# A written order of single steps for the last stage's first tiles, a raw row's scale from its maximum, and column sums moved into the expert products

## The chip, the cores and the metric

One core of one Trainium2 chip runs the whole program in one launch. The metric is the device time of an execution in microseconds. Engines in the text: PE is the matrix engine (its weight loads are shown as PEld), DVE, ACT and POOL work elementwise, SP issues the DMAs.

## The reference

Three computations follow each other. Pooled attention over 8 heads gives `x` (4608 rows of 512). A soft mixture of 8 experts takes `x` to 32 slots, sends each slot through its expert's two layers, and mixes the slots back to rows. The last part, which the change touches, works row by row on that mixture `x`:

```python
h = x @ w_in
e = np.exp(h - h.max(axis=-1, keepdims=True))
solu = h * (e / (e.sum(axis=-1, keepdims=True) + 1e-09))
mu = solu.mean(axis=-1, keepdims=True)
var = ((solu - mu) ** 2).mean(axis=-1, keepdims=True)
return ((solu - mu) / np.sqrt(var + 1e-06) * g_ln) @ w_out
```

`w_in` is 512 by 1024, `w_out` 1024 by 512, both given in double precision.

## The kernel before

**Stages.** Attention with the slot sums takes the program to about 170 us; the second expert layer follows (line L847, sixteen slots of four matmuls, two per expert, each slot waiting for its weights from DMA); then the slots are multiplied with `w_in` once (L893 to L917), so that a row of the last stage needs one short product. The last stage treats the 4608 rows as 36 tiles of 128 rows.

**A tile of the last stage.** PE makes `h` (128 by 1024) from the mixing weights `cS` and the matrix `MS`; DVE finds the maximum `nm`; ACT takes the exponential `e` and its sum; DVE multiplies `u = h * e` and sums it; POOL and ACT work out mean and variance; `u` is brought to its normed form `v`, split into a high and a low f16 part (`vhi`, `vlo`), and laid with the 1024 columns on the partitions. Then PE makes 24 matmuls of 128 by 512 per tile: 8 chunks of `vhi` with `W_hi` and with `W_lo` (L1137, L1138), and 8 of `vlo` with `W_hi` (L1140). `W_hi` and `W_lo` are the two f16 parts of `w_out` with `g_ln`.

**Three kinds of tile.** Tiles 0 to 2 are "raw" (functions `raw_*`): their `u` is turned on PE before mean and variance are known, and the mean's part is put right at the end with the column sums of W. Those sums are made by `out_sums` (L1074, L1075: for each of 8 chunks one matmul of a matrix of ones with `W_hi` and one with `W_lo`) and kept by ACT in `csum`. A raw tile's `u` is scaled to fit f16 by `raw_scale`, which runs two more maximum reductions over `h`, of absolute values (L999), and three operations on one column (L1000 to L1002). Tile 3 is normed first and then turned on PE (L1044 to L1047). From tile 4 on the f16 parts are turned by DMA: SP issues one transposing DMA for `vhi` and one for `vlo` (L1129), and each finished block of three tiles leaves by a 768 KB output DMA (L1159) from the same SP queue.

**What sets the order.** Most of the program is ordered by a scheduler at build time. From the end of the expert products the order is written by hand in the string `steps`: each name is an operation declared with `op` and the names that it needs. In before the steps reach whole functions: `F3` is all of tile 3's front from `h` to its statistics, `G3` its turning, `P0a` both parts of four chunks of tile 0's products. The fixed order holds up to the step `E`; the operations behind it, and all later tiles, are again put in order by the scheduler. The names of the steps: f h's matmul, x maximum, k scale, e exponential, u product with h, t turning on PE, h (with two digits) the high part, w the low part, m mean, v squares, d statistics, P products, R output rows, p S T the copies of M that make `MS`, o column sums; the first digit is the tile, the second the half.

**Dummy matmuls.** Slots 9 to 14 of the expert products are each followed by one matmul of 128 by 512 into a tile that nobody reads (`DUM`, `spare`, L876).

Of the kernel before, what the change touches and what calls it, by code (L numbers as in the profile page):

```python
# [19 lines left out]
P = 128  # L20
# [65 lines left out]
def moe_attention_kernel(ctx: ExitStack, tc, q, k, v, phi, w1, w2, w_in, w_out, g, out):  # L86
# [639 lines left out]
    if True:  # L726
# [114 lines left out]
        DUM = {9: (512,), 10: (512,), 11: (512,), 12: (512,), 13: (512,), 14: (512,)}  # L841
        if DUM:
            spare = psE.tile([P, DM], F32, name="spare")
# [8 lines left out]
        CE = (0, 0, 0, 2, 9, 11, 12, 12, 13)  # L852
        CI = {3: (("o", 2),), 4: (("o", 3),), 6: (("i", 0),), 7: (("i", 1),), 11: (("i", 2),)}
# [29 lines left out]

        t1 = {}
# [67 lines left out]
    BF = dict(e=2, u=3, v=2, h1=2, h2=2, s=4, hi=4)  # L952
# [13 lines left out]
    csum = T_all.rearrange("p g s -> p (g s)")  # L966
# [74 lines left out]
    def split_turned(v, hi, lo, hf):  # L1041
        pu = ps2.tile([P, 4, P], F32, tag="vT", name="vT")
        for c in range(4):
            pe.transpose(pu[:, c, :], v[:, P * c:P * c + P], ident)  # L1044
        hd = hi[:, 4 * hf:4 * hf + 4, :]
        act.activation(hd, pu, AF.Copy)  # L1046
        dve.tensor_tensor(lo[:, 4 * hf:4 * hf + 4, :], pu, hd, ALU.subtract)  # L1047

    def raw_mean(i):
        hs, nm, u, e, st = u_t[i]  # L1050
        y = rs_t[i] = wk2.tile([P, 4], F32, name="y0", bufs=2)
        pool.tensor_tensor(y[:, 0:1], st[:, 2:3], st[:, 3:4], ALU.add)
        pool.tensor_scalar(y[:, 0:1], y[:, 0:1], -1.0 / DF, None, ALU.mult)
# [16 lines left out]
    def out_sums(c):  # L1070
        if c == 0:
            t1["pcs"] = ps2.tile([P, DM], F32, tag="o", name="pcs")
        pcs = t1["pcs"]
        pe.matmul(pcs, ones_h, W_hi[:, c, :], start=(c == 0), stop=False)  # L1074
        pe.matmul(pcs, ones_h, W_lo[:, c, :], start=False, stop=(c == NFC - 1))  # L1075

    def out_sums_kept():
        act.activation(csum, t1["pcs"], AF.Copy)

    def front(i):  # L1080
# [15 lines left out]
        z = wk2.tile([P, 3], F32, name="z", bufs=BF["s"])
# [7 lines left out]
        u_t[i] = u, nmu, sr  # L1104
        r = rs_t[i] = wk2.tile([P, 1], F32, name="r", bufs=BF["s"] + 1)
        pool.tensor_scalar(r, sr[:, 1:2], sr[:, 2:3], ws[:, 2:3], ALU.mult, ALU.mult)  # L1106

    def turn(i):

        u, nmu, sr = u_t.pop(i)  # L1110
        hi, lo = (wk2.tile([P, NFC, P], F16, name=x, bufs=BF["hi"]) for x in ("vhi", "vlo"))
        hi_t[i], lo_t[i] = hi, lo
        v = wk2.tile([P, DF], F32, name="v", bufs=BF["v"])
        if V == "act":
            b = wk2.tile([P, 1], F32, name="b", bufs=BF["s"])
            pool.tensor_tensor(b, nmu, sr[:, 0:1], ALU.mult)  # L1116
            act.activation(v, u, AF.Identity, bias=b, scale=sr[:, 0:1])  # L1117
        else:
            dve.tensor_scalar(v, u, nmu, sr[:, 0:1], ALU.add, ALU.mult)
        if i < NPT:  # L1120
            for hf in range(2):
                split_turned(v[:, 512 * hf:512 * hf + 512], hi, lo, hf)
            return
        v1 = wk2.tile([P, DF], F16, name="v1", bufs=BF["h1"])
        v2 = wk2.tile([P, DF], F16, name="v2", bufs=BF["h2"])
        dve.tensor_scalar(v1, u, nmu, sr[:, 0:1], ALU.add, ALU.mult)  # L1126
        eng[H2].tensor_tensor(v2, v, v1, ALU.subtract)  # L1127
        for src, dst in ((v1, hi), (v2, lo)):
            sp.dma_start_transpose(out=dst, in_=src)  # L1129
# [12 lines left out]
    def rows_out(i):  # L1142
        po = po_t.pop(i)
# [48 lines left out]
    for m in range(NRAW, NT):  # L1192
        for j in range(NRAW + 3, m + LAG + 1) if m == NRAW else (m + LAG,):
            if j < NT:
                front(j)
            if NRAW + 3 <= j - 1 < NT:
                turn(j - 1)
# [59 lines left out]
```

## Time and profile before

| what | value |
|---|---|
| median of 3 runs | 445.54 us (444.97 to 446.08) |
| span of the profiled execution | 444.7 us |
| PE busy in the span | 90% |
| DVE, ACT, POOL busy | 72%, 67%, 52% |
| first matmul of tile 0's `h` | 222.42 us |
| first of tile 0's products | 232.36 us |
| last matmul | about 441.4 us |

The profiled execution is known by its span alone, 444.7 us from the first to the last instruction; the median of the runs is 0.8 us above it. Times in the views count from the span's start. A timeline row gives the start, the length, the instruction and, in brackets, how long the engine stood idle ahead of it and what ended that wait. The ends of matmuls are modelled, so that neighbouring rows overlap: the time that PE needs for one is the distance between starts.

### The profile page before, as it was taken

To read this page: it belongs to the slowest core of one execution; us is meant where nothing else is said; L and a number is where in the kernel's file an instruction comes from. 1 tells how busy PE (TensorE), PEld (TensorE's weight loads), DVE (VectorE), ACT (ScalarE), POOL (GpSimd) and SP (SyncE) were. 2 spreads that over 40 slices of the span, in tenths; PEclk is the share of its full clock that TensorE was granted. 3 is DMA by queue.
4 is the path that set the end of the run, shared out by engine and by line. 5 is a ranking of instruction groups with operands and counts; after the bars stand their busy time and mean duration, and the time that the engine had idled before them with its cause. 6 is when DMAs were issued, how large, how long until landed. Compare 5 with 4: busy or idle time off the path is not lost. (4 is left out here: it accounts for less than half of the span.)

```text
span 444.7 us, 8298 instructions
## 1 busy us (share of the span) xinstructions
PE 398.7 (90%) x2983; PEld 231.1 (52%) x2983; DVE 320.1 (72%) x519; ACT 299.2 (67%) x664; POOL 229.7 (52%) x427
## 2 busy tenths in 40 slices
PE   4679988987999797868789999999999999999997
PEld 4667867866977424321234544444444444444445
DVE  4897897798873624788379887778888887878610
ACT  3588987767795505765338867778887887777721
POOL 5498776568331026773213556665555555555510
PEclk9899998999899887998999999999999999999999
DMA  8999999673779797899300065777765786665661
GB/s 253 412 396 418 398 413 363 228 251 132 277 276 341 260 326 288 330 420 422 151 1 1 16 150 112 150 166 113 172 165 96 177 177 105 147 158 106 151 165 47
DMA packets 87800, 97.07 MB, mean 218 GB/s; under 512 B 70096, under 2 KB 74960, under 8 KB 82768
## 3 DMA queue, kind: packets, MB, share of 16 engines
q1 hardware_dynamic: 87760, 96.55, 69.3%
q8 instruction: 23, 0.38, 0.3%
q14 instruction: 17, 0.14, 0.1%
HBM read 70.32 MB, written 9.44 MB: 179 GB/s over the span
## 5 line engine op out<-in xcount | busy, mean ns | idle before, releaser
L1137 PE MATMUL o<-W_hi,vhi 128*128 128x512 f16 x280 | 106.4, 380 | 1.1 <-ACT vhi L1046 1.0
L1138 PE MATMUL o<-W_lo,vhi 128*128 128x512 f16 x280 | 106.1, 379 | 0.0
L1140 PE MATMUL o<-W_hi,vlo 128*128 128x512 f16 x280 | 67.3, 379 | 0.5 <-DVE vlo L1026 0.5
L366 PE MATMUL sc<-BD,qT 128*128 128x144 f32 x320 | 53.4, 316 | 13.8 <-ACT BD L307 7.8
L366 PEld LDWEIGHTS sc<-BD,qT 128*128 128x128 f32 x320 | 47.3, 212 | 16.3 <-POOL sel L264 6.6
L1117 ACT ACTIVATE v<-u,b,sr 128x1024 f32<-128x1024 f32 x33 | 40.9, 1239 | 15.0 <-POOL b L1116 14.6
L1137 PEld LDWEIGHTS <-vhi 128*128 128x128 f16 x280 | 27.3, 98 | 38.9 <-issue 7.5
L1127 DVE TENSOR_TENSOR v<-v,v 128x1024 f16<-128x1024 f32 x32 | 39.2, 1224 | 10.8 <-ACT v L1117 10.6
L1094 ACT ACTIVATE e<-u,nmu 128x1024 f32<-128x1024 f32 x33 | 37.9, 1148 | 13.4 <-POOL nmu L1093 12.9
L1089 ACT ACTIVATE e<-h,nm 128x1024 f32<-128x1024 f32 x33 | 36.6, 1110 | 13.5 <-DVE nm L1086 13.3
L1140 PEld LDWEIGHTS <-vlo 128*128 128x128 f16 x280 | 27.2, 98 | 33.5 <-DVE vlo L1026 1.0
L405 POOL TENSOR_TENSOR a<-a,rs 128x864 f32<-128x864 f32 x23 | 37.7, 1649 | 13.1 <-DVE rs L403 6.9
L1138 PEld LDWEIGHTS <-vhi 128*128 128x128 f16 x280 | 27.4, 98 | 30.1 <-issue 0.9
L1091 DVE CUSTOM_DVE_ANT_0 u<-h,e 128x1024 f32<-128x1024 f32 x33 | 40.3, 1222 | 3.7 <-ACT e L1089 3.4
L1086 DVE TENSOR_REDUCE nm<-h 128x1 f32<-128x1024 f32 x33 | 40.1, 1220 | 3.9 <-PE h L1083 3.8
L1126 DVE TENSOR_SCALAR v<-u,nmu,sr 128x1024 f16<-128x1024 f32 x32 | 26.0, 812 | 18.8 <-POOL sr L1103 18.7
L411 PE MATMUL pt<-ident,a 128*128 128x128 f32 x180 | 30.8, 287 | 4.5 <-ACT aT L417 3.0
L377 DVE TENSOR_REDUCE nmax<-sc 128x6 f32<-128x432 f32 x48 | 28.1, 597 | 6.4 <-PE sc L366 6.0
L417 ACT ACTIVATE aT<-pt 128x384 f32<-128x384 f32 x60 | 28.0, 491 | 6.7 <-PE pt L411 6.3
L1106 POOL TENSOR_SCALAR r<-sr,ws 128x1 f32<-128x1 f32 x33 | 29.1, 881 | 3.4
L1103 POOL TENSOR_TENSOR sr<-z,exponents 128x3 f32<-128x3 f32 x33 | 28.9, 875 | 2.7
L1153 ACT ACTIVATE ob<-o,r 128x512 f32<-128x512 f32 x32 | 21.4, 669 | 9.6 <-PE o L1140 9.6
(238 smaller groups left out, 764.4 us busy)
## 6 DMA issues: line engine op xcount, KB each, us to landing
w<-in_w_dram SPq DMA_DIRECT2D x16, 1024.0 KB, 10.0
vT<-in_v_dram SPq DMA_DIRECT2D x8, 1152.0 KB, 14.7
out_dram<-ob SPq DMA_DIRECT2D x11, 768.0 KB, 3.7
w<-in_w_dram SPq DMA_DIRECT2D x16, 512.0 KB, 5.7
kT<-in_k_dram SPq DMA_DIRECT2D x7, 1152.0 KB, 13.7
qT<-in_q_dram SPq DMA_DIRECT2D x7, 768.0 KB, 14.3
qT<-in_q_dram SPq DMA_DIRECT2D x8, 384.0 KB, 16.7
raw<-in_w_in_dram SPq DMA_DIRECT2D x3, 1024.0 KB, 9.5
```

The costliest lines, as they stand in the source:

```text
L366: pe.matmul(sc[:, r].rearrange("p h j -> p (h j)"), qT[n][:, hp, x, :], BD[b % NBD][:, hp, :], start=(i == 0), stop=(i == len(hv) - 1))
L405: eng.tensor_tensor(av, av, rs.unsqueeze(3).to_broadcast([P, NR, 4, J]), ALU.mult)
L411: pe.transpose(pt[:, r, :], a_buf[n % NA][:, r, CH[c]:CH[c] + P], ident)
L1086: dve.tensor_reduce(nm, hv, axis=AX.X, op=ALU.max, negate=True)
L1089: act.activation(e, hv, AF.Exp, bias=nm, accum_out=st[:, 0:1])
L1091: dve.tensor_tensor_reduce(u, hv, e, 1.0, 0.0, ALU.mult, ALU.add, st[:, 1:2])
L1094: act.activation(e, u, AF.Square, bias=nmu, accum_out=st[:, 2:3])
L1117: act.activation(v, u, AF.Identity, bias=b, scale=sr[:, 0:1])
L1127: eng[H2].tensor_tensor(v2, v, v1, ALU.subtract)
L1137: pe.matmul(po, hi[:, c, :], W_hi[:, c, :], start=(c == 0), stop=False)
L1138: pe.matmul(po, hi[:, c, :], W_lo[:, c, :], start=False, stop=False)
L1140: pe.matmul(po, lo[:, c, :], W_hi[:, c, :], start=False, stop=(c == NFC - 1))
```

## The change

It has four parts.

1. `out_sums` moves from the last stage into the expert products: chunks 0 to 5 are written behind slots 12, 13 and 14, where the dummy matmuls of these slots go; chunk 6 and 7 and the copy into `csum` become steps between the end of the expert products and the making of `MS`.
2. `raw_scale` takes the scale from the maximum that is already there (`nm`) and not from two reductions of absolute values.
3. The functions of tiles 3 to 9 are cut into single steps (`front_pe`, `front_max`, and so on; the steps `Fa` to `Fg`, `Ga` to `Gy`), the products of tiles 0 to 2 into high parts (`P0a`, `P0b`), which need only `vhi`, and low parts (`P0al`, `P0bl`). A new string `steps` writes out their order up to tile 3's products, where `E` now stands, and the fronts up to tile 9.
4. Three buffers for `e` where two were, three for `y0` where two were.

```diff
-        DUM = {9: (512,), 10: (512,), 11: (512,), 12: (512,), 13: (512,), 14: (512,)}
+        DUM = {9: (512,), 10: (512,), 11: (512,)}
...
+        CS = {12: (0, 1), 13: (2, 3), 14: (4, 5)}
...
                 pe.matmul(spare[:, 0:nn], ident, w2t[x // 2, x % 2, 3][:, 0:nn], start=True, stop=True)
+            for c in CS.get(x, ()):
+                out_sums(c)
...
+        for c in (6, 7):
+            op(f"o{c}", f"o{c - 1}" if c > 6 else "", out_sums, c)
+        op("csum", "o7", out_sums_kept)
...
+        steps = ('a0 o6 a1 s0 s1 s2 s3 o7 so i0 i1 M0 M1 csum N0 mh0 N1 mh1 X '
+                 'f00 f01 p0 S0 x00 x01 k0 p1 e00 e01 S1 T0 u00 f10 t00 u01 h00 t01 h01 T1 P0a w00 x10 m0 f11 w01 x11 k1 e10 e11 P0al '
...
-    BF = dict(e=2, u=3, v=2, h1=2, h2=2, s=4, hi=4)
+    BF = dict(e=3, u=3, v=2, h1=2, h2=2, s=4, hi=4)
...
     def raw_scale(i):
 
         hs, nm, u, e, st = u_t[i]
-        am = wk2.tile([P, 2], F32, name="am", bufs=2)
-        for hf in range(2):
-            dve.tensor_reduce(am[:, hf:hf + 1], hs[hf], axis=AX.X, op=ALU.max, apply_absolute_value=True)
-        dve.tensor_tensor(am[:, 0:1], am[:, 0:1], am[:, 1:2], ALU.max)
-        dve.tensor_scalar(am[:, 0:1], am[:, 0:1], 1e-30, 2.0 ** -14, ALU.max, ALU.mult)
-        dve.reciprocal(st[:, 4:5], am[:, 0:1])
+        am = wk2.tile([P, 1], F32, name="am", bufs=2)
+        dve.tensor_scalar(am, nm, -1.0, nm, ALU.mult, ALU.max)
+        dve.tensor_scalar(am, am, 1.0, 2.0 ** -14, ALU.max, ALU.mult)
+        dve.reciprocal(st[:, 4:5], am)
...
-    def products(i, c0, c1):
+    def products(i, c0, c1, what="hl"):
...
-        for c in range(c0, c1):
+        for c in range(c0, c1) if "h" in what else ():
             pe.matmul(po, hi[:, c, :], W_hi[:, c, :], start=(c == 0), stop=False)
             pe.matmul(po, hi[:, c, :], W_lo[:, c, :], start=False, stop=False)
-        for c in range(c0, c1):
+        for c in range(c0, c1) if "l" in what else ():
             pe.matmul(po, lo[:, c, :], W_hi[:, c, :], start=False, stop=(c == NFC - 1))
...
-        op(f"P{i}a", f"w{i}0", products, i, 0, 4)
-        op(f"P{i}b", f"w{i}1 P{i}a", products, i, 4, 6)
-        op(f"P{i}c", f"P{i}b", products, i, 6, 8)
+        op(f"P{i}a", f"h{i}0", products, i, 0, 4, "h")
+        op(f"P{i}al", f"w{i}0 P{i}a", products, i, 0, 4, "l")
+        op(f"P{i}b", f"h{i}1 P{i}al", products, i, 4, 8, "h")
+        op(f"P{i}bl", f"w{i}1 P{i}b", products, i, 4, 8, "l")
```

**PE, the last slots of the expert products.** `p_2401` is the tile that gathers the expert products, `w_60` to `w_74` the weights of slots 12 to 15, `spare` the dummies, `pcs` the column sums, `ps` the first matmuls behind the experts. Before, the slots and the dummies alternate:

```order
L847 MATMUL p_2401<-w_54_2331,hTm 32x512 x4
L876 MATMUL spare<-w_54_2331,ident 128x512
L847 MATMUL p_2401<-w_60_2335,hTm 32x512 x4
L876 MATMUL spare<-w_60_2335,ident 128x512
L847 MATMUL p_2401<-w_64_2337,hTm 32x512 x4
L876 MATMUL spare<-w_64_2337,ident 128x512
L847 MATMUL p_2401<-w_70_2339,hTm 32x512 x4
L876 MATMUL spare<-w_70_2339,ident 128x512
L847 MATMUL p_2401<-w_74_2341,hTm 32x512 x4
L893 MATMUL ps<-sel_73,s_2620 128x32 x4
```

With the change seven groups like the first four rows here, chunks 0 to 6 of the sums, stand together between the dummy of slot 11 and slot 12 (chunk 7 comes behind `ps`):

```order
L848 LDWEIGHTS ones_h
L848 MATMUL pcs<-W_hi,ones_h 128x512
L849 LDWEIGHTS ones_h
L849 MATMUL pcs<-W_lo,ones_h 128x512
L856 MATMUL p_2401<-w_60_2335,hTm 32x512 x4
L856 MATMUL p_2401<-w_64_2337,hTm 32x512 x4
L856 MATMUL p_2401<-w_70_2339,hTm 32x512 x4
L856 MATMUL p_2401<-w_74_2341,hTm 32x512 x4
L904 MATMUL ps<-sel_73,s_2630 128x32 x4
```

So the scheduler has put the sums ahead of slot 12, also those that the code writes behind slots 12 to 14, and nothing stands between the last four slots.

**DVE, tile 0 in the last stage.** `h_2662` and `h_2663` (now `h_2677` and `h_2678`) are the halves of tile 0's `h`, `pM` the copies of M that make `MS`, ISA is the product `u`. Before:

```order
L985 TENSOR_REDUCE nm_2669<-h_2662 128x1
L1037 TENSOR_TENSOR MS<-pM_2664,MS 64x512
L985 TENSOR_REDUCE nm_2669<-h_2663 128x1
L988 TENSOR_TENSOR nm<-nm_2669 128x1
L1037 TENSOR_TENSOR MS<-pM_2665,MS 64x512
L999 TENSOR_REDUCE am<-h_2662 128x1
L999 TENSOR_REDUCE am<-h_2663 128x1
L1000 TENSOR_TENSOR am<-am 128x1
L1001 TENSOR_SCALAR am<-am 128x1
L1002 RECIPROCAL st<-am 128x1
L1011 ISA u,st<-h_2662,e,st 128x512
```

With the change:

```order
L1004 TENSOR_REDUCE nm_2685<-h_2677 128x1
L1004 TENSOR_REDUCE nm_2685<-h_2678 128x1
L1007 TENSOR_TENSOR nm<-nm_2685 128x1
L1017 TENSOR_SCALAR am<-nm 128x1
L1018 TENSOR_SCALAR am<-am 128x1
L1019 RECIPROCAL st<-am 128x1
L1054 TENSOR_TENSOR MS<-pM_2679,MS 64x512
L1028 ISA u,st<-h_2677,e,st 128x512
L1028 ISA st 128x1
L1028 ISA u,st<-h_2678,e,st 128x512
```

The two reductions into `am` are gone from between the maxima and the first `u`, and of the two operations that make `MS` one stands ahead of the first `u` and one behind the second.

## Rows read from the trace of the kernel before

**Rows 1.** The page, part 1: busy us of each engine, share, instructions.

```profile
PE 398.7 (90%) x2983; PEld 231.1 (52%) x2983; DVE 320.1 (72%) x519; ACT 299.2 (67%) x664; POOL 229.7 (52%) x427
```

**Rows 2.** By stretch: length, PE, PEld, DVE, ACT, POOL busy, PEclk, DMA, GB/s.

```profile
222.40:232.40 10.00, 7.97 (x32) 3.77 (x32) 7.54 (x18) 3.83 (x8) 1.02 (x5) 1.00 0.01 2
232.40:256.30 23.90, 22.37 (x113) 11.74 (x112) 21.18 (x41) 20.24 (x38) 11.76 (x44) 1.00 0.04 17
256.30:284.40 28.10, 28.01 (x129) 12.98 (x130) 23.07 (x27) 20.23 (x30) 16.62 (x41) 1.00 0.68 138
284.40:441.40 157.00, 156.96 (x744) 75.20 (x743) 111.76 (x129) 110.18 (x158) 80.64 (x206) 1.00 0.66 140
```

**Rows 3.** Waits of PE from 222 to 444 us: total us, times, longest us.

```profile
PE pu L1017 <- DVE st L1011: 2.0, 1, 2.0
PE o L1137 <- ACT vhi L1046: 1.0, 1, 1.0
PE o L1140 <- DVE vlo L1026: 0.5, 1, 0.5
```

**Rows 4.** Timeline of PE, last stage: start, us, instruction, idle before, releaser.

```profile
222.42 1.13 PE L978 MATMUL h<-hTm,c_first 128*128 128x512 f32 x2
230.33 1.33 PE L1017 MATMUL pu<-ident,u 128*128 128x128 f32 x8 [2.01 <-DVE st L1011]
232.36 0.38 PE L1137 MATMUL o<-W_hi,vhi 128*128 128x512 f16 x1
256.30 0.39 PE L1137 MATMUL o<-W_hi,vhi 128*128 128x512 f16 x1 [0.99 <-ACT vhi L1046]
```

**Rows 5.** Timeline of PE: two neighbouring matmuls of the column sums.

```profile
225.96 0.38 PE L1074 MATMUL pcs<-W_hi,ones_h 128*128 128x512 f16 x1
226.17 0.38 PE L1075 MATMUL pcs<-W_lo,ones_h 128*128 128x512 f16 x1
```

**Rows 6.** Timeline of DVE: tile 0's scale and the first half of its u.

```profile
223.58 0.69 DVE L985 TENSOR_REDUCE nm<-h 128x1 f32<-128x512 f32 x1 [2.19 <-PE h L978]
227.51 1.29 DVE L999 TENSOR_REDUCE am<-h 128x1 f32<-128x512 f32 x2
229.22 0.16 DVE L1002 RECIPROCAL st<-am 128x1 f32<-128x1 f32 x1
229.52 0.75 DVE L1011 CUSTOM_DVE_ANT_0 u<-h,e,st 128x512 f32<-128x512 f32 x1
```

**Rows 7.** Timeline of ACT: first copy of MS, first exponential of tile 0.

```profile
224.44 0.60 ACT L1033 ACTIVATE MS<-pM 128x512 fp32r<-128x512 f32 x1 [1.32 <-PE pM L1030]
228.24 0.69 ACT L1006 ACTIVATE e<-h,nm 128x512 f32<-128x512 f32 x1 [1.49 <-DVE am L999]
```

**Rows 8.** Timeline of PE among the expert products.

```profile
198.92 0.83 PE L811 MATMUL pc<-ident,c 128*128 128x128 f32 x4 [2.10 <-DVE cS L816]
199.69 1.94 PE L847 MATMUL p<-w,hTm 128*32 128x512 f32 x8
207.00 1.07 PE L847 MATMUL p<-w,hTm 128*32 128x512 f32 x8 [1.76 <-DMA w<-in_w_dram]
209.48 1.07 PE L847 MATMUL p<-w,hTm 128*32 128x512 f32 x8 [0.36 <-DMA w<-in_w_dram]
214.49 1.06 PE L847 MATMUL p<-w,hTm 128*32 128x512 f32 x8 [0.39 <-DMA w<-in_w_dram]
```

**Rows 9.** PE alone by stretch: length, busy, PEclk, DMA share, GB/s.

```profile
195.00:199.00 4.00, 1.90 (x11) 1.00 1.01 414
199.00:202.50 3.50, 3.50 (x13) 0.53 1.03 426
227.00:231.00 4.00, 1.98 (x10) 1.00 0.00 0
```

**Rows 10.** DMA issues, median us to landing: from 277 to 280 us; whole run.

```profile
vhi<-v SPq DMA_TRANSPOSE x1, 4.2
vhi<-v SPq DMA_TRANSPOSE x32, 3.1
```

More of the change, by code (lines that the diff above doesn't have):

```diff
@@ L928, in moe_attention_kernel @@
             op(f"mh{hf}", f"N{hf}", m_high, hf)
-        steps = ('a0 a1 s0 s1 s2 s3 so i0 i1 M0 M1 N0 mh0 N1 mh1 X f00 p00 S0 x00 T0 f01 p10 S1 x01 T1 o0 o1 k0 f10 e00 u00 e01 u01 o2 o3 f11 x10 t00 t01 x11 k1 '
-                 'h00 e10 w00 o4 h01 u10 o5 m0 w01 P0a e11 t10 f20 f21 v0 u11 d0 x20 P0b o6 o7 P0c t11 E csum x21 k2 R0 h10 e20 e21 u20 '
-                 'm1 t20 u21 v1 t21 h21 F3 F4 h11 m2 w10 h20 w11 P1a w20 d1 P1b P2a P1c R1 G3 v2 d2 w21 P2b G4 P2c F5 G5 R2').split()
+        for c in (6, 7):
+            op(f"o{c}", f"o{c - 1}" if c > 6 else "", out_sums, c)
+        op("csum", "o7", out_sums_kept)
+        steps = ('a0 o6 a1 s0 s1 s2 s3 o7 so i0 i1 M0 M1 csum N0 mh0 N1 mh1 X '
[5 rows of a table added]
+                 'Gy6 R4 Fe9 Ga7 P5a Ff9 P5bl Gc7 Ff8 R5 Gx7 Fg8 Fg9 Ga8 Gb8 Gy7 Gx8 Gc8 Gy8 K1').split()
         assert sorted(set(steps)) == sorted(steps)
@@ L1039, in moe_attention_kernel @@
     pu_t = {}
[L1041 to L1047, printed above, removed]
     def raw_mean(i):
         hs, nm, u, e, st = u_t[i]
[L1051 removed]
+        y = rs_t[i] = wk2.tile([P, 4], F32, name="y0", bufs=3)
         pool.tensor_tensor(y[:, 0:1], st[:, 2:3], st[:, 3:4], ALU.add)
@@ L1068, in raw_stats, with front_pe @@
         pool.tensor_tensor(y[:, 0:1], y[:, 0:1], y[:, 1:2], ALU.mult)
[L1070 to L1080, printed above, removed]
+    ft = {}
+    def front_pe(i):
         ph2 = ps2.tile([P, 2, 512], F32, tag="h", name=f"h{i}")
@@ L1103, in front @@
         pool.tensor_tensor(sr, z, exps_, ALU.pow)
-        u_t[i] = u, nmu, sr
+        b = wk2.tile([P, 1], F32, name="b", bufs=BF["s"])
+        pool.tensor_tensor(b, nmu, sr[:, 0:1], ALU.mult)
+        u_t[i] = dict(u=u, nmu=nmu, sr=sr, b=b)
         r = rs_t[i] = wk2.tile([P, 1], F32, name="r", bufs=BF["s"] + 1)
         pool.tensor_scalar(r, sr[:, 1:2], sr[:, 2:3], ws[:, 2:3], ALU.mult, ALU.mult)
-    def turn(i):
[L1110 to L1129, printed above, removed]
@@ L1131, in products, with front, turn_scale, turn_pe @@
-    def products(i, c0, c1):
+    def front(i):
+        for f in (front_pe, front_max, front_exp, front_u, front_mean, front_square, front_stats):
+            f(i)
+    def turn_scale(i):
+        u, nmu, sr, b = (u_t[i][x] for x in ("u", "nmu", "sr", "b"))
+        v = u_t[i]["v"] = wk2.tile([P, DF], F32, name="v", bufs=BF["v"])
+        act.activation(v, u, AF.Identity, bias=b, scale=sr[:, 0:1])
+    def turn_pe(i, hf):
+        v = u_t[i]["v"]
+        pu = pu_t[i, hf] = ps2.tile([P, 4, P], F32, tag="vT", name="vT")
+        for c in range(4):
+            pe.transpose(pu[:, c, :], v[:, 512 * hf + P * c:512 * hf + P * c + P], ident)
+        if hf == 0:
+            hi_t[i], lo_t[i] = (wk2.tile([P, NFC, P], F16, name=x, bufs=BF["hi"]) for x in ("vhi", "vlo"))
@@ new lines, in turn_high, with turn_low, turn_high_out @@
+    def turn_high(i):
+        u, nmu, sr = (u_t[i][x] for x in ("u", "nmu", "sr"))
+        v1 = u_t[i]["v1"] = wk2.tile([P, DF], F16, name="v1", bufs=BF["h1"])
+        dve.tensor_scalar(v1, u, nmu, sr[:, 0:1], ALU.add, ALU.mult)
+    def turn_low(i):
+        v2 = u_t[i]["v2"] = wk2.tile([P, DF], F16, name="v2", bufs=BF["h2"])
+        dve.tensor_tensor(v2, u_t[i]["v"], u_t[i]["v1"], ALU.subtract)
+    def turn_high_out(i):
+        hi_t[i], lo_t[i] = (wk2.tile([P, NFC, P], F16, name=x, bufs=BF["hi"]) for x in ("vhi", "vlo"))
+        sp.dma_start_transpose(out=hi_t[i], in_=u_t[i]["v1"])
@@ L1132, in products, with turn_low_out @@
+    def turn_low_out(i):
+        sp.dma_start_transpose(out=lo_t[i], in_=u_t.pop(i)["v2"])
+    def turn(i):
+        for f in (turn_scale, turn_high, turn_high_out, turn_low, turn_low_out):
+            f(i)
+    def products(i, c0, c1, what="hl"):
         hi, lo = hi_t[i], lo_t[i]
-        if c0 == 0:
+        if c0 == 0 and "h" in what:
             po_t[i] = ps2.tile([P, DM], F32, tag="o", name=f"o{i}")
         po = po_t[i]
-        for c in range(c0, c1):
+        for c in range(c0, c1) if "h" in what else ():
@@ L1159, in rows_out @@
             sp.dma_start(out[blk], o_t.pop(blk).rearrange("p r d -> p (r d)"))
+    def rows_out(i):
+        rows_scaled(i)
+        if i < NRAW:
+            rows_sum(i)
+        rows_kept(i)
     for hf in range(2):
-        op(f"p{hf}0", f"mh{hf}", m_copies, hf, 0)
-        op(f"S{hf}", f"p{hf}0", ms_high, hf)
+        op(f"p{hf}", f"mh{hf}", m_copies, hf, 0)
+        op(f"S{hf}", f"p{hf}", ms_high, hf)
         op(f"T{hf}", f"S{hf}", ms_low, hf)
-    for c in range(NFC):
-        op(f"o{c}", f"o{c - 1}" if c else "", out_sums, c)
-    op("csum", f"o{NFC - 1}", out_sums_kept)
     for i in range(NRAW):
@@ L1191, in moe_attention_kernel @@
     assert not ops, ops.keys()
[L1192 to L1197, printed above, removed]
+    for m in range(NPRO, NT):
+        j = m + LAG
+        if j < NT:
+            front(j)
+        if j - 1 < NT:
+            turn(j - 1)
         if m < NT - 1 or not LS:
```

80 lines of the change are left out of this document (62 added, 18 removed), and 4 rows, old and new, of the table steps.

## Prediction

> **What bounds the kernel now.** The page's busy times come first: PE leads with 90% of the span [rows 1], but that is a mean over stages. So the next view is the busy time by stretch of the last stage [rows 2]. From 284.4 to 441.4 us PE is busy in 156.96 of 157.0 us, DVE in 111.8 and ACT in 110.2; from 256.3 to 284.4 it is much the same. There PE is the bound, and the reader should see what follows from it: if PE comes to tile 3's products earlier, with the same work behind it, the end comes earlier by as much. Only the opening, 222.4 to 256.3, has room: PE is busy 7.97 + 22.37 = 30.3 of 33.9 us, so 3.6 us are idle. The view of PE's waits names them [rows 3]: 2.0 us for DVE's first `u`, 1.0 for tile 3's `vhi`, 0.5 for tile 0's `vlo`, and no other that matters. The timeline of PE gives the marks [rows 4]: first `h` at 222.42, turning of tile 0 from 230.33, first product at 232.36, first of tile 3's products at 256.30. Ahead of that last mark stand the fronts of tiles 3 to 7 in before and in the new order alike, so the mark can be compared directly. The prediction is the shift of this mark, and then what changes on either side of it.
>
> **The sums leave PE's opening.** There are 8 chunks of 2 matmuls, and two neighbours start 0.21 to 0.22 us apart [rows 5]: 16 x 0.215 = 3.4 us of PE's work leave the stretch. Where they go they are cheap. PE ended its dummy of slot 11 at 207.00 - 1.76 = 205.24 and then waited for weights [rows 8]. Now 14 matmuls (3.0 us) run there to 208.25, and slot 12, 1.0 us long, to 209.25. Slot 13 began at 209.48 because its weights came then, so the 1.25 us by which slot 12 is late are absorbed, at no cost; without that wait they would cost all of 1.25. The last pair (0.43 us) runs while DVE copies the slots, the copy into `csum` in an idle stretch of ACT; both at nothing, and 0.4 at most.
>
> **The opening's chain, walked along the new order.** `f00` starts at 222.42 as before and `f01` follows at 223.3 (four f32 matmuls lie between 222.42 and 225.96, 0.88 each [rows 4, 5]). Its half of the maximum takes 0.69 [rows 6] and ends at 225.1, so `nm` stands at 225.3. The scale was two reductions (1.29 us) and small operations that ended with the reciprocal at 229.38 [rows 6]; now it is three operations on one column, 0.16 long and some 0.2 apart, done at 225.9. On ACT the first copy of `MS` (0.60) now runs 225.3 to 225.9 and the exponential (0.69) right behind it, where it stood at 228.24 [rows 7]. Its first half and sum are ready at 226.8, so `u` starts there, 2.7 us ahead of its 229.52 [rows 6]. The turning starts at 227.5 in place of 230.33, ACT makes the high part behind its second copy of `MS`, and since the high products no longer wait for `vlo` nor stand behind two pairs of sums, they start at 228.9 in place of 232.36 [rows 4]: 3.4 us earlier.
>
> Along that walk PE stands idle 0.75 us for `T0` (behind `f10` stand the turnings, which wait for `u` anyway), 0.6 for `u00`, 0.3 for `u01` and `h00`. Walked on in the same way to tile 3, it waits 0.3 at `Fa3`, whose PSUM buffer is freed by `u11`, 0.3 at `t20` for `u20`, and 0.1 elsewhere: 2.4 us. Before it was 3.6. The stretch becomes 30.3 - 3.4 + 2.4 = 29.3 us, tile 3's products start at 251.7, **4.6 us earlier**. Bounds: only the first three waits, which the chain forces, give 5.3 earlier; waits as large as before give 3.4. I take the walk's value, because its first waits rest on rows and the later ones are small.
>
> **What else is moved.** The single steps issue the same instructions as the functions did, so they cost nothing by themselves; what covers them is that DVE and ACT keep up. DVE loses 3 x 1.3 = 3.9 us of reductions: of its 7.54 + 21.18 = 28.7 us in the opening [rows 2] 24.8 are left for 29.3 us, 85% as before; ACT has 24.1 of 29.3, 82%. If that cover went, rival C would be the case. A third buffer for `e` only takes waits away.
>
> Behind `E` PE meets tile 4's and tile 5's high products, then their low ones. Tile 5's `vhi` is issued on SP behind the first output block; a transposing DMA next to an output took 4.2 us to land, the median is 3.1 [rows 10]. By the same walk DVE has made that tile's f16 part at about 257.8, so it lands at 260.9 to 262.0; PE comes there at 251.7 + 24 x 0.215 + two fronts of 2 x 0.215 + 16 x 0.215 = 261.2, all by the distance in [rows 5]. The wait is 0 to 0.8, and I take **0.3**, nearer to the lower end, since the median lies there. Later tiles have more slack than this one.
>
> **The clock.** Three dummies go, and by the order the sums don't replace them: slots 12 to 15 stand bare. From 209.48 on each slot is 1.0 us of work, one per 2.5 us as the weights come, since 214.49 - 209.48 is two slots [rows 8], so PE idles 1.5 us between them where a dummy stood. [...] But ahead of 230.33 it had waited 2.0 us, and the clock stayed at 1.00 [rows 4, 9]. [...] Slot 15 is on the path: ACT's copy, DVE's words of the last part of `w_in` and `h` all follow it. Price: 1.94 - 1.07 = 0.9 us. [...] I take **0.9**.
>
> **Sum.** -4.6 + 0.3 + 0.9 = -3.4 us. The profiled execution's span of 444.7 becomes 441.3. The median of the runs, 445.54, is 0.84 above that span, so the forecast is **442.1 us**.
>
> **Rivals.**
>
> A: the clock stays up. Speaking for it is the wait ahead of 230.33, against it the one ahead of 198.92. Sum -4.6 + 0.3 = -4.3, time 441.2. [...]
>
> B: the whole opening fits, clock and DMA cost nothing, and only the forced waits stay: -5.3, below 440.3.
>
> C: DVE and ACT set the opening's pace. They are at 85% and 82%, and each engine takes its steps in the written order only: where DVE waits for an exponential of tile 4 (`Fd4`), the low part and output of tiles 1 and 2 stand queued behind it, and PE waits for those. Some 1.2 us more at each of two tiles turn the forecast into 444.5; with one, 443.3.
>
> D, slower: the same queueing, but growing. The written order is rigid from `f00` to tile 3; if DVE's and ACT's waits for each other took their use from 85% down to 70%, 24.8 us of DVE's work would need 35.4, the mark would come at 257.8 and the time be 447.0. That is the point from which it decides. Against it: the walk finds no wait of DVE over 0.7 us once tile 0's `u` is made.
>
> E: the change does not do what it says. In part that is so already, since the sums stand ahead of slot 12; were they to hold up slot 15, they would have to be late by 1.25 us and the slack at 209.48 more, and nothing in the rows shows that.
>
> **How the numbers follow.** Forecast 0.45, A 0.35, B 0.04, C 0.12, D 0.03, E 0.01. The range leaves out B, half of C, D and E: from 440.3 (A with its DMA wait at nothing and the walk's later waits gone by half) to 443.9 (the forecast with the clock's price at 1.7 and one such wait of 1.0). About 0.3%, 1.3 us, is what a measurement can tell from no change here: 444.2 to 446.9. Slower is D and E, 0.04. Within is the upper part of C, 0.07. Faster is the rest, 0.89.
>
> **What would show it.** In the profile of after: the first product of tile 0 near 229 us, or 230 with the clock's fall; the first of tile 3 near 251.7, or 252.6; PE's waits between them about 2.4 us in total, the longest for `T0` and `u00`; no matmul of the column sums behind 218 us; the granted clock between 212 and 218, which decides between the forecast and A; PE busy without gaps from tile 6 on. The prediction is wrong if PE's waits ahead of tile 3 add up to 3.6 or more, if a wait of over 1 us for `vhi` or `vlo` stands at tiles 4 to 9, or if slot 15 ends later than 216.5.

## The result and the profile after

The change makes the kernel **slower**: 448.65 us median (445.10 to 453.02, 20 runs) against 443.06 (440.42 to 448.5, 20 runs), a ratio of 1.010 with a 95% interval of 1.0073 to 1.0127. The ratio leaves out the runs that lie over 1.5% above the fastest of their kernel, so it is a little smaller than that of the medians. The profiled execution has a span of 446.9 us; before it was 444.7. Forecast were 442.1 us, against the 445.54 of the three runs known then, and a range of 440.3 to 443.9, with 0.04 for slower.

The busy times tell little: PE has 1.4 us less to do than in [rows 1], and yet the span is longer, so PE waits more.

```profile
PE 397.3 (89%) x2977; PEld 230.8 (52%) x2977; DVE 314.6 (70%) x513; ACT 296.9 (66%) x664; POOL 236.8 (53%) x427
```

The view of PE's waits from 222 to 444 us, the stretch of [rows 3] (us in total, times, longest), says for what:

```profile
PE o L1174 <- ACT ob L1187: 4.9, 13, 0.9
PE h L994 <- DVE nm L1004: 1.4, 2, 1.1
PE pu L1034 <- ACT vhi L1040: 0.7, 1, 0.7
PE h L994 <- DVE MS L1054: 0.6, 1, 0.6
PE pu L1034 <- DVE st L1028: 0.3, 1, 0.3
```

The last four rows are the opening's, 3.0 us together. The first is new: 13 times PE stands ahead of a tile's first product until ACT has copied out the products of the tile two before, since the tag `o` has two PSUM buffers. The busy time by stretch (columns as in [rows 2]) tells where:

```profile
251.80:313.70 61.90, 61.79 (x285) 28.86 (x284) 48.98 (x60) 46.07 (x67) 41.76 (x91) 1.00 0.68 148
313.70:441.40 127.70, 122.75 (x572) 58.19 (x571) 83.34 (x97) 83.09 (x122) 63.03 (x157) 1.00 0.61 133
```

Up to 313.7 us PE is full as it was before; from there on it lacks 5 us, where [rows 2] had 0.04 in 157. A tile, from one front's matmuls to the next one's, takes 5.66 us up to 313.7 and 5.98 in the mean behind it. The opening itself went much as forecast. The marks of [rows 4] again:

```profile
221.48 1.98 PE L997 MATMUL h<-hTm,c_first 128*128 128x512 f32 x4
226.59 0.65 PE L1034 MATMUL pu<-ident,u 128*128 128x128 f32 x4 [0.29 <-DVE st L1028]
228.43 0.38 PE L1174 MATMUL o<-W_hi,vhi 128*128 128x512 f16 x1
251.78 0.38 PE L1174 MATMUL o<-W_hi,vhi 128*128 128x512 f16 x1
```

From the first `h` to tile 0's first product 6.95 us (9.94 before), to tile 3's 30.30 us (33.88). Ahead of that, among the expert products (the place of [rows 8]), something was lost:

```profile
206.37 1.95 PE L856 MATMUL p<-w,hTm 128*32 128x512 f32 x16
209.74 1.06 PE L856 MATMUL p<-w,hTm 128*32 128x512 f32 x8 [1.43 <-DMA w<-in_w_dram]
212.25 1.06 PE L856 MATMUL p<-w,hTm 128*32 128x512 f32 x8 [1.44 <-DMA w<-in_w_dram]
213.82 1.90 PE L904 MATMUL ps<-sel,s 128*128 128x32 f32 x8 [0.50 <-ACT s L901]
216.50 5.04 PE L924 MATMUL pM<-win,so 128*32 128x512 f32 x16
```

PE now waits 1.43 us ahead of slots 14 and 15, and behind slot 15 the granted clock falls: 0.73 from 212 to 216 us, 0.50 from 216 to 219, 0.72 to 222. From slot 15's start to the first `h` it takes 9.23 us, before 7.93.

When slot 15 starts depends on the weights' pace: 208.3 to 215.3 us over the profiled executions of all kernels here. Two of the kernel before have 214.49 and 211.58, and each then needs 230.2 us to its end. So the profiles are compared from slot 15's start on, in three pieces (marks of PE's timeline, and the span):

| kernel | slot 15 to first `h` | to tile 3's first product | to the end | sum |
|---|---|---|---|---|
| before | 7.93 | 33.88 | 188.4 | 230.2 |
| changed | 9.23 | 30.30 | 195.1 | 234.6 |
| difference | +1.3 | -3.6 | +6.7 | +4.4 |

4.4 us of 445 are 1.0%, which is the measured ratio. The gain is there, and it is paid back almost twice in the steady part, where the prediction saw nothing happen.

### The profile page after: what moved, and what is told of

The parts are those of the page before. It is cut to its first block, busy times and chain, and to the rows that moved or that the text cites. A ratio compares the mean times of both kernels' runs of the same rounds, so it can differ in the third digit from the quotient of the medians.

```text
span 446.9 us, 8280 instructions
## 1 busy us (share of the span) xinstructions
PE 397.3 (89%) x2977; PEld 230.8 (52%) x2977; DVE 314.6 (70%) x513; ACT 296.9 (66%) x664; POOL 236.8 (53%) x427
## 5 line engine op out<-in xcount | busy, mean ns | idle before, releaser
L1155 DVE TENSOR_TENSOR v<-v,v 128x1024 f16<-128x1024 f32 x32 | 39.1, 1223 | 10.0 <-ACT v L1138 9.8
L1151 DVE TENSOR_SCALAR v<-u,nmu,sr 128x1024 f16<-128x1024 f32 x32 | 26.0, 813 | 26.4 <-POOL sr L1124 26.4
L1177 PEld LDWEIGHTS <-vlo 128*128 128x128 f16 x280 | 27.2, 98 | 32.3 <-issue 0.3
L411 PEld LDWEIGHTS pt<-ident,a 128*128 128x128 f32 x180 | 21.3, 147 | 9.4 <-ACT aT L417 3.1
L389 ACT ACTIVATE a<-dd 128x432 f32<-128x432 f32 x36 | 19.8, 567 | 9.2 <-DVE ssum L396 4.7
```

The source lines that it names most:

```text
L411: pe.transpose(pt[:, r, :], a_buf[n % NA][:, r, CH[c]:CH[c] + P], ident)
L1155: dve.tensor_tensor(v2, u_t[i]["v"], u_t[i]["v1"], ALU.subtract)
```

## The experiments

**The suspect in the tail.** The steps of the statistics were regrouped: POOL now multiplies `b` (v's bias) directly behind the power `sr`, at L1126, and `r` behind it, at L1129. In the kernel before `b` was part of `turn` and came behind `r`. On ACT the build's order in the main loop was one tile long before (copy, exp, v, Square); in the changed kernel it repeats only every third tile. So the first set put `b` back, made the same swap in the kernel before, and treated the clock separately.

```
 # front_stats(i), changed kernel
+        pool.tensor_scalar(r, sr[:, 1:2], sr[:, 2:3], ws[:, 2:3], ALU.mult, ALU.mult)
         pool.tensor_tensor(b, nmu, sr[:, 0:1], ALU.mult)
-        pool.tensor_scalar(r, sr[:, 1:2], sr[:, 2:3], ws[:, 2:3], ALU.mult, ALU.mult)
```

> The changed kernel with one edit: in the stages' statistics POOL computes b (for v) behind r again, as in the kernel before; the written order, the third buffer of e and the moved sums stay. Theory (b ahead of r let the scheduler put ACT's instructions behind tile 5 into an order of three tiles, in which a v and an exp or a Square stand ahead of the copy that frees the products' PSUM bank): ACT's order is one tile long again, PE's wait for the copy is gone, the stretch from tile 3's first product to the end falls from 195.1 us to 188 to 189.5, a tile takes 5.66 us throughout, and the time falls by 5.5 to 7 us against the changed kernel: ratio to before 0.988 to 0.996. Rival 1 (the written opening or the third buffer of e leaves the tail in a bad state): that stretch stays at 194 us or more, ratio 1.007 to 1.013. Rival 2 (the clock's fall behind slot 15 and its effects): the same, ratio 1.007 to 1.013.

Measured: 442.86 us, ratio 0.9948 (0.9906 to 0.999). The pieces are 9.64, 30.3 and 188.4 us. This is as expected. The tail is that of the kernel before, and from the first `h` on PE's waits are the opening's alone.

> The kernel before with the one edit the other way: b is computed ahead of r on POOL, all else as before. Theory: the tail takes the order of three tiles, PE waits about 0.4 us a tile for the copy that frees the products' bank on some 13 tiles and the stretch from tile 3's first product (188.4 us in the kernel before) grows by 4 to 7 us: ratio 1.008 to 1.016. Rivals 1 and 2: nothing but two tiny POOL operations has changed places, the time stays within 0.3%: ratio 0.997 to 1.003.

Measured: 452.65 us, ratio 1.0203 (1.0143 to 1.0262), more than forecast; pieces 7.93, 33.7, 196.1. PE's first wait there:

```profile
PE o L1137 <- ACT ob L1153: 5.9, 15, 1.2
```

So the swap of two POOL instructions, of 0.2 and 0.3 us, makes the loss by itself. With `b` first the build puts ACT and DVE into an order of three tiles in this kernel too; with it behind, in the run above, into the order of one tile. The clock's part:

```
-        DUM = {9: (512,), 10: (512,), 11: (512,)}
+        DUM = {9: (512,), 10: (512,), 11: (512,), 12: (512,), 13: (512,), 14: (512,)}
```

> The changed kernel with the three matmuls that keep PE busy while it waits for slots 12 to 14 put back; b stays ahead of r. Theory: they give back at most what the clock's fall behind slot 15 costs, 1.3 us (first h 9.2 us behind slot 15's start instead of 7.9); the waits for the copy in the tail stay; ratio to before 1.005 to 1.012. Rival 2 (the clock is the cause): the granted clock behind slot 15 is 1.00 again and the whole loss goes: ratio 0.988 to 0.996. Rival 1: as the theory.

> The changed kernel with both edits: b behind r and the three matmuls back. Theory: the two gains add, 5.5 to 7 us and up to 1.3 us: ratio to before 0.985 to 0.994, and below the first run of this set by up to 0.3%. Rival 1: 1.005 to 1.012. Rival 2: the same as with the matmuls alone, 0.988 to 0.996.

Measured: 1.0164 (1.0105 to 1.0224) and 0.9974 (0.9933 to 1.0015). Both lie above what was expected. The clock stayed at 1.00 from slot 15 to the first `h`, but this was no clean test of its price: with the dummies back the build put the 14 sums behind slot 15, where they stand on the path, and slot 15 to the first `h` took 10.28 us in both. In the first of the two the clock then fell at tile 0's first products, to a mean of 0.57 from 226 to 230 us, and its middle piece is 31.4 us where it is 30.3 in the other. The tail is 195.2 with `b` first and 188.2 with it behind. That `b` decides the tail holds; the dummies gave nothing.

**Which mechanism.** I took ACT's order for the cause. So the next run kept `b` first and held ACT's order as it was before (`after` sets an order on one engine; E is the exp, S the Square, o the copy, j = m + 4).

```
             rows_out(m)
+            if j < NT:
+                for x, y in ((("E", j), ("v", j - 1)), (("v", j - 1), ("S", j)), (("S", j), ("o", m))):
+                    after(act_i[x], act_i[y])
```

> The changed kernel with b still ahead of r on POOL, but with ACT's instructions in the main loop held in the order exp of tile j, v of j-1, Square of j, copy of tile m's products. Theory (what costs is ACT's order; two tiny POOL operations that change places cost nothing by themselves): PE's waits for the copy are gone, a tile takes 5.66 us throughout, 5.5 to 7.5 us below the changed kernel: ratio to before 0.990 to 0.999. Rival (POOL itself is late: r or b comes too late for the copy or for v, whatever ACT's order): PE still waits about 0.4 us on each tile, ratio 1.006 to 1.014.

Measured: 449.19 us, ratio 1.0173 (1.0145 to 1.0201). **The theory fell**: with the one-tile order in place PE waits on 20 tiles, 6.6 us in all, and every tile behind 312 us takes 6.09 us. But that makes the loop easy to read. The timeline of all engines there, over one tile:

```profile
363.24 0.81 DVE L1151 TENSOR_SCALAR v<-u,nmu,sr 128x1024 f16<-128x1024 f32 x1 [1.86 <-POOL sr L1124]
363.29 0.19 POOL L1126 TENSOR_TENSOR b<-nmu,sr 128x1 f32<-128x1 f32 x1
363.46 0.81 POOL L1129 TENSOR_SCALAR r<-sr,ws 128x1 f32<-128x1 f32 x1
363.51 1.24 ACT L1138 ACTIVATE v<-u,b,sr 128x1024 f32<-128x1024 f32 x1 [0.23 <-POOL b L1126]
363.97 1.22 DVE L1102 CUSTOM_DVE_ANT_0 u<-h,e 128x1024 f32<-128x1024 f32 x1
365.11 1.22 DVE L1155 TENSOR_TENSOR v<-v,v 128x1024 f16<-128x1024 f32 x1
365.29 1.12 POOL L1108 TENSOR_SCALAR nmu<-st 128x1 f32<-128x1 f32 x1 [0.46 <-DVE st L1102]
366.44 1.15 ACT L1113 ACTIVATE e<-u,nmu 128x1024 f32<-128x1024 f32 x1 [1.69 <-POOL nmu L1108]
```

`nmu`, one column, takes 1.12 us; it ends at 366.41, and DVE's `v2` (L1155), which had begun 0.18 earlier, at 366.33. `r`, begun 0.22 us behind the start of `v1` (L1151), takes 0.81 in place of 0.34. `b`, begun 0.05 us behind that start, takes its usual 0.19. The same place in the first experiment:

```profile
364.35 0.81 DVE L1151 TENSOR_SCALAR v<-u,nmu,sr 128x1024 f16<-128x1024 f32 x1 [1.02 <-POOL sr L1124]
364.43 0.87 POOL L1126 TENSOR_SCALAR r<-sr,ws 128x1 f32<-128x1 f32 x1
365.26 0.18 POOL L1128 TENSOR_TENSOR b<-nmu,sr 128x1 f32<-128x1 f32 x1
365.48 1.24 ACT L1138 ACTIVATE v<-u,b,sr 128x1024 f32<-128x1024 f32 x1 [0.91 <-POOL b L1128]
366.40 0.23 POOL L1108 TENSOR_SCALAR nmu<-st 128x1 f32<-128x1 f32 x1 [0.40 <-DVE st L1102]
366.66 1.15 ACT L1113 ACTIVATE e<-u,nmu 128x1024 f32<-128x1024 f32 x1
366.75 1.23 DVE L1155 TENSOR_TENSOR v<-v,v 128x1024 f16<-128x1024 f32 x1 [0.45 <-ACT v L1138]
```

Here `r` sits out `v1`, so `b` comes late, ACT's v comes late, and `v2`, which subtracts from v, starts 0.45 us after DVE is free. In that gap `nmu` gets through in 0.23 us. With `b` first `v2` is ready as soon as `u` is done, 0.18 us ahead of `nmu`. The groups of instructions from 284 to 420 us (count | busy us, mean ns | idle before), for before, changed, ACT's order held:

```profile
L1093 POOL TENSOR_SCALAR nmu<-st 128x1 f32<-128x1 f32 x26 | 9.6, 370 | 13.8 <-DVE st L1091 13.8
```
```profile
L1108 POOL TENSOR_SCALAR nmu<-st 128x1 f32<-128x1 f32 x23 | 13.2, 574 | 11.5 <-DVE st L1102 11.5
```
```profile
L1108 POOL TENSOR_SCALAR nmu<-st 128x1 f32<-128x1 f32 x22 | 24.7, 1125 | 10.5 <-DVE st L1102 10.5
```

By the single rows 4 of 26, 9 of 23 (in the mean every 18 us, on each third tile) and all 22 began under a `v2` and took 1.1 to 1.3 us; every other one took 0.22 (the texts below say 24 for the 22, by a double count). `v2` has two inputs in SBUF, and the `nmu` in the rows above ends 0.08 us behind it. Under `v1` `r` goes the same way, ending 0.22 us behind it, and `b`, which begins 0.05 us behind `v1`'s start, doesn't: it ends 0.57 us ahead of `v1`'s end. So the rows show when POOL is held up and for how long; what in `v2` and `v1` does it stays open.

In the run with ACT's order held this loop sets the pace: Square 366.44, statistics, `v1` at 369.33, `u` at 370.06, `nmu` 371.38 to 372.51, next Square 372.54, 6.1 us a tile. With a `nmu` of 0.22 it would be 5.2, an estimate, below PE's 5.66. In the changed kernel only each third `nmu` is late, and in this order of one tile that would fit: 5.2 + 5.2 + 6.1 = 16.5 us for three tiles, where PE needs 17.0. But there DVE's and ACT's orders repeat every three tiles. One `v2` stands ahead of the next `u`, and one `u` waits for an exp that stands behind a Square:

```profile
348.99 1.15 ACT L1113 ACTIVATE e<-u,nmu 128x1024 f32<-128x1024 f32 x1 [1.39 <-POOL nmu L1108]
353.40 1.23 DVE L1155 TENSOR_TENSOR v<-v,v 128x1024 f16<-128x1024 f32 x1 [0.72 <-ACT v L1138]
354.54 1.22 DVE L1102 CUSTOM_DVE_ANT_0 u<-h,e 128x1024 f32<-128x1024 f32 x1
358.48 1.23 DVE L1102 CUSTOM_DVE_ANT_0 u<-h,e 128x1024 f32<-128x1024 f32 x1 [1.58 <-ACT e L1096]
365.78 1.12 POOL L1108 TENSOR_SCALAR nmu<-st 128x1 f32<-128x1 f32 x1 [0.61 <-DVE st L1102]
366.94 1.15 ACT L1113 ACTIVATE e<-u,nmu 128x1024 f32<-128x1024 f32 x1 [1.39 <-POOL nmu L1108]
```

From the first Square to the last, three tiles on, it is 17.95 us, 5.98 a tile. Less the 0.9 us of the late `nmu` it would be 17.05, 5.7 a tile: an estimate from these rows, since no run freed `nmu` in this order. So the order of three tiles uses up the room, and the late `nmu` makes the loss. The tiles that stand ready are used up by 313 us, and from then on PE pays. The chain of waits (start, us, what) shows the last such place in the changed kernel:

```profile
419.65 1.13 POOL nmu L1108
420.83 1.03 issue
422.05 0.58 ACT ob L1187
422.68 0.38 PE o L1174
```

Two runs test this, each against the run with ACT's order held. One computes `nmu` (n) on DVE behind `u` and holds DVE's order of the large instructions (1 is `v1`, 2 `v2`, M the max); the other leaves `nmu` on POOL and puts the next tile's max between `u` and `v2`.

```
-        pool.tensor_scalar(nmu, st[:, 1:2], -1.0 / DF, None, ALU.mult)
+        dve.tensor_scalar(nmu, st[:, 1:2], -1.0 / DF, None, ALU.mult)
...
-                for x, y in (..., (("S", j), ("o", m))):
+                for x, y in (..., (("S", j), ("o", m)), (("n", j), ("2", j - 1)), (("o", m - 1), ("E", j)), (("2", j - 2), ("M", j))):
```

> The kernel of the run with ACT's order held (b ahead of r, 6.09 us a tile), with one instruction on another engine: nmu, which ACT's Square waits for, is computed on DVE directly behind u instead of on POOL; DVE's order of the large instructions (v1, u, v2, next max) and ACT's are held as they were in that run. Theory now (POOL can't run while DVE's v2 runs: all 24 nmu there began under a v2 and took 1.12 us, 0.22 us otherwise, and the loop Square, statistics, v1, u, nmu, Square is then 6.09 us long): the loop is about 0.7 us shorter, PE's 20 waits for the copy go, a tile takes 5.66 us; ratio to before 0.990 to 0.999. Rival (b ahead of r on POOL, or ACT's order, holds the copy or v up by itself): waits and 6.09 us stay, ratio 1.012 to 1.020.

```
-                for x, y in (..., (("S", j), ("o", m))):
+                for x, y in (..., (("S", j), ("o", m)), (("o", m - 1), ("E", j)), (("M", j), ("2", j - 2)), (("2", j - 2), ("1", j - 1))):
```

> The same kernel with nmu left on POOL and b ahead of r, but DVE's v2 put behind the next tile's max instead of ahead of it; ACT's order is held as before. Theory now: the max reads PSUM, and the nmu that began under a max took 0.22 us, so nmu takes 0.22 us on all tiles, PE's waits for the copy go and a tile takes 5.66 us; ratio to before 0.990 to 1.000. Rival (not v2 but POOL's own order is what costs): nmu's place and length change nothing, 6.09 us a tile, ratio 1.012 to 1.020.

Measured: 440.54 us, ratio 0.9939 (0.9903 to 0.9974), and 441.66 us, 0.9986 (0.9945 to 1.0027). In both `b` is first and ACT's order is the one that had 6.09; in both a tile takes 5.66 us. PE waits once for the copy in the one (0.7 us) and never in the other. Its timeline, where the max, with its source in PSUM, doesn't hold `nmu` up (0.22 us):

```profile
364.06 1.22 DVE L1089 TENSOR_REDUCE nm<-h 128x1 f32<-128x1024 f32 x1
364.23 0.22 POOL L1108 TENSOR_SCALAR nmu<-st 128x1 f32<-128x1 f32 x1 [0.47 <-DVE st L1102]
364.49 1.15 ACT L1113 ACTIVATE e<-u,nmu 128x1024 f32<-128x1024 f32 x1 [0.79 <-POOL nmu L1108]
365.19 1.22 DVE L1155 TENSOR_TENSOR v<-v,v 128x1024 f16<-128x1024 f32 x1
```

So in the order of one tile `b`'s place costs nothing by itself; `nmu` under `v2` does. For the changed kernel's order of three tiles, its share is the estimate above.

**The sums and the clock.** The sums, held behind their own slots in a bank of their own, each group with a short dummy, on top of `b` behind `r`:

```
-        DUM = {..., 11: (512,)}
+        DUM = {..., 11: (512,), 12: (128,), 13: (128,), 14: (128,)}
-                out_sums(c)
+                after(slot_, out_sums(c))
```

> The first experiment's kernel (b behind r) with the column sums held behind the expert products that they were written behind: four matmuls after slots 12 and 13, six after slot 14, two in the step behind slot 15, in a PSUM bank of their own, each group with one matmul of 128 columns that keeps PE busy as before. Theory on the opening (14 sums in one block ahead of slot 12 leave PE waiting 1.1 to 1.4 us for each later slot, the granted clock falls to half, and slot 15's start to the first h takes 9.2 to 9.6 us instead of 7.9): that stretch is 7.9 to 8.3 us, and the time falls by 1.2 to 1.8 us against the first experiment: ratio to before 0.988 to 0.993. Rival (the sums cost the slots as much as they free, or the clock falls anyway): ratio 0.993 to 0.999, the stretch 9 us or more.

> The kernel with b behind r and the sums in the gaps a second time, beside the one before it on the same chip: its span from the first h to the last front was 188.56 us (192.14 in the kernel before) and slot 15 to the first h 7.92 us (7.93), so 3.6 us are to be gained if the rest of the program is equal: ratio 0.988 to 0.996; the first measurement gave 0.9977 (0.9939 to 1.0014).

Measured: 441.13 us, 0.9977 (0.9939 to 1.0014), then 440.16 us, 0.9933 (0.9892 to 0.9974). From slot 15 to the first `h` it takes 7.92 and 7.93 us, as before the change:

```profile
207.66 1.06 PE L857 MATMUL p<-w,hTm 128*32 128x512 f32 x8
210.15 1.06 PE L857 MATMUL p<-w,hTm 128*32 128x512 f32 x8
212.86 1.06 PE L857 MATMUL p<-w,hTm 128*32 128x512 f32 x8
214.43 1.08 PE L906 MATMUL ps<-sel,s 128*128 128x32 f32 x8 [0.50 <-ACT s L903]
```

The sums then cost the slots nothing but the 0.2 us of the last group. The first ratio lies above what was expected, the second within. The sum from slot 15 is 226.6 and 227.7 us, 3.6 and 2.5 below before. The second has 31.4 us in the middle piece, like three other profiles with the new opening (31.3 to 31.4, the other six 30.3). In all four the clock fell for some 3 us at tile 0's first products, here to a mean of 0.57 from 226 to 230 us, and in none of the six. Of these four executions two had slots 12 to 15 bare and two had sums or dummies there. So this is a fall of its own, at some 1.1 us, that comes in some executions; what brings it on stays open. With `nmu` on DVE in addition:

> The kernel with nmu on DVE, and the column sums held in the gaps between the expert products with the short busy matmuls. Theory: 5.66 us a tile and 7.9 to 8.3 us from slot 15's start to the first h; ratio to before 0.986 to 0.996, within 0.4% of the run after this. If PE is the bound behind the opening there, nmu on DVE gives nothing over b behind r.

Measured: 0.9961 (0.9918 to 1.0004), sum 227.4 us. Nothing more to gain, as PE is the bound either way.

**Parts alone.** In the kernel before, first the sums among the expert products, with the three dummies gone, then the scale's source:

```
+            for c in CS.get(x, ()):
+                out_sums(c)
```

> The kernel before with the column sums moved among the expert products as in the changed kernel (the three matmuls that kept PE busy go), nothing else. By the prediction's first term the 3.4 us of the sums leave the opening and slot 12 waits anyway: ratio 0.991 to 0.994. Theory now: the sums that stood in the opening filled PE while it waited for the first u (2.0 us) and for ACT's and DVE's halves, so less than 2 us of them comes off the path to tile 3's products, and the stretch from slot 15 to the first h grows by 1.3 to 1.7 us: ratio 0.996 to 1.003.

```
-        for hf in range(2): dve.tensor_reduce(am[:, hf:hf + 1], hs[hf], ..., apply_absolute_value=True)
+        dve.tensor_scalar(am, nm, -1.0, nm, ALU.mult, ALU.max)
```

> The kernel before with the raw row's scale taken from its maximum, nothing else. By the prediction two reductions of 1.29 us for three tiles leave DVE, of which about 1 us lies on the path of the first u: ratio 0.996 to 1.000. Theory of the scheduled tail: the other durations in the opening shift the state from which the scheduler orders the tail; ACT's order there has two exps, two Squares and two vs in a row on about 10 tiles, so PE waits for the copy or for the turned rows there: ratio 1.002 to 1.010.

Measured: 1.0141 (1.0097 to 1.0184) and 1.0101 (1.0063 to 1.0139). Both lie above what was expected. The sums alone: pieces 9.15, 34.1, 188.4, so nothing is gained in the opening (before 33.88). Of the 3.4 us of PE's work that left it, about half comes back as waits: 5.4 us in all where [rows 3] had 3.6, the longest 2.3 for the first `u`, where the sums stood. The other half goes to the clock, which fell to 0.50 from 230.9 to 234.2 us, at tile 0's first products. The scale alone: 7.93, 32.3, 192.3; 1.6 gained in the opening, 3.9 lost behind tile 3, with only 1 of 24 `nmu` late. That tail is another one: its fronts come in pairs, and up to 345 us PE waits 1.6 us for the copy and 0.8 for turned rows from DMAs. That is not taken apart further.

Both measured above what their profiles give (231.6 and 232.5 us against 230.2). Four more profiles asked why.

> A second profile of the kernel before with the sums moved alone, whose runs (447.7 us median, 445.75 to 451.5) lie above what its profile tells (slot 15's start to the end 231.6 us against 230.2 in the kernel before, so a ratio of about 1.003). If the tail falls into the collisions in some executions only (nmu under v2 on more than 8 tiles), slot 15 to the end is 234 us or more here; if the spread lies ahead of slot 15 (the weights' pace), it is 231.6 us within 0.5 and only slot 15's start moves.

> A third profile of the same kernel, with the same two expectations: 234 us or more from slot 15's start to the end with nmu under v2 on more than 8 tiles, or 231.6 us within 0.5.

> A second profile of the kernel before: slot 15's start to the end 230.2 us within 0.5 if the tail is the same in each execution and the spread of the times (439 to 448 us) lies ahead of slot 15; more than 1 us away if the tail itself falls into two states.

> A second profile of the kernel before with the scale's source changed alone (1.0101 measured; its first profile gives 232.5 us from slot 15's start to the end against 230.2, about 1.005): 232.5 us within 0.5 if the tail is the same in each execution, 234 us or more if not.

From slot 15 on: 231.8 and 233.9 us for the sums alone, 230.2 for before, 232.4 for the scale alone. From tile 3's first product to the end each kernel takes the same within 0.1 us in its profiled executions. What varies is slot 15's start (208.3 to 215.3 us in these four) and, with the sums alone, how long the clock stays low at the first products: 3 to 4 us in two of its three profiled executions, and 10 us, from 227 to 237, in the one with 233.9. The rest of the difference between ratio and profile stays open.

## Why the prediction was wrong, step by step

- **"so they cost nothing by themselves; what covers them is that DVE and ACT keep up"** is the step that failed. The single steps do issue the same instructions, but not in the same places: `b` passed `r` on POOL, and I neither named that nor priced POOL at all. With `b` first `v2` gets ahead of `nmu` on each third tile, the build orders DVE and ACT by three tiles, and the tail loses 6.7 us.
- **The premise that what PE gains ahead of tile 3 is gained at the end** rests on PE being the bound behind it in [rows 2]. PE was, but with 0.5 us of room in a loop through ACT, POOL and DVE (5.2 against 5.66). A delay of 0.9 us on every tile turns that round (6.09), and so does one on each third tile in an order that has no room left (5.98). With `b` put back the premise holds: 188.4 us from tile 3 on, as before.
- **The opening's walk**, -4.6 us to tile 3's products: measured -3.6, inside its bounds (3.4 to 5.3) and near the lower. PE's waits there are 3.0 us where the walk had 2.4, the longest (1.1) for DVE's `nm` of a raw tile, which it didn't have. That the marks themselves came near (228.43 and 251.78 us, forecast 229 and 251.7) is luck: slot 15 began 2.2 us earlier in this execution.
- **The sums at no cost** held among the slots: behind the block PE still waited 1.43 us for slot 14's weights. **The clock's term**, for the slots that this left bare, was mis-sized: 0.9 forecast, 1.3 measured, and 1.7 in the run with `b` put back. That the clock would fall there at all was my estimate from two waits, with 0.53 behind the one and 1.00 behind the other [rows 4, 8, 9]. The 0.9, the difference of two slots' times in [rows 8], was an estimate as well, and so was the 1.7 in the range's upper end; no run shows the 0.9, the runs showed 1.2 to 1.7 us more from slot 15 to the first `h` (9.15 to 9.64 against 7.93).
- **Tile 5's wait**, +0.3: not there; the tail with `b` put back is equal to that of before.
- With these sizes and without `b`'s move, -3.6 + 1.7 = -1.9 us, and that run measured 0.9948, some 2.3 us below before.
- **The rivals**: D foresaw "slower" by queueing in the opening, and the opening was faster; C likewise. A was wrong on the clock. No rival had the tail. Of the signs only "PE busy without gaps from tile 6 on" looked there, and it failed; none of the three that were to show the prediction wrong came. The range's lower end is also mis-added: by its own terms it is 440.6, not 440.3, which changes nothing.

## What to carry to other kernels

When a function is cut into steps, compare the order of each engine with the old one, the small engines too: an instruction of 0.2 us that passes another can decide which of two large ones comes first. A tiny instruction with two lengths in a trace (0.22 and 1.2 us here, already in the kernel before: mean 370 ns) may be one that something blocks; find out what, and ask what happens if it is blocked each time. And a bound read from busy times has a margin, which is the length of the next loop: work that out before saying that a gain ahead of it reaches the end.

## What the runs showed of the hardware

Each POOL instruction on one column that began under DVE's `v2` (two SBUF inputs) ended only behind it: `nmu` 0.07 to 0.09 us behind, 1.12 to 1.30 us long instead of 0.22. Under `v1` (SBUF to SBUF) `r`, which began 0.07 us or more behind `v1`'s start, was held in the same way (0.80 to 0.90 us instead of 0.34, and 1.92 where `v2` followed at once), while `b`, where it began at most 0.05 us behind it, took its 0.19. Under DVE's max (from PSUM) and under `u` (one input in PSUM) none was held: `nmu` took 0.22 to 0.23 us, `b` 0.18 to 0.19.

TensorE's granted clock fell behind slot 15 in the changed kernel, which leaves slots 12 to 15 bare, with waits of 1.43 and 1.44 us ahead of slots 14 and 15: to 0.73 from 212 to 216 us and to 0.50 from 216 to 219. Slot 15 to the first `h` took 9.23 us there, and, with the slots as bare, 9.64 with `b` put back and 9.15 to 9.24 in three executions with the sums alone: 1.2 to 1.7 more than the 7.93 of before. With the max ahead of `v2`, where these slots are bare too, the clock stayed at 1.00 from 209.5 to 217.6 us. With dummies between the slots it stayed at 1.00 in the kernel before from 214 to 222.4 us, and with sums and a short dummy there from 212.8 to 221.

It also fell at tile 0's first products: to 0.57 in the mean from 226 to 230 us in one run with dummies and in one with sums in the gaps, to 0.53 from 225 to 228 with the max ahead of `v2`, to 0.50 from 230.9 to 234.2 with the sums alone, and in another execution of that kernel for 10 us, from 227 to 237, with two neighbouring products 0.43 us apart instead of 0.215.
